# An attention and two-FFN kernel: gate and value of batch 1 from seven products a block instead of eight, and the sums of weights that they need made from the output product of batch 0 on

## The chip, the cores and the metric

The kernel runs on one core of a Trainium2 chip. Its time is the device time of one launch in microseconds (us). Five engines work beside each other, each on its own queue of instructions in a fixed order: TensorE (PE in the profile, its weight loads PEld), VectorE (DVE), ScalarE (ACT), GpSimd (POOL) and SyncE (SP), which here issues the transfers. They wait for each other by semaphores.

## The reference

The reference is an attention with a memory, followed by two feed-forward stages on 4 batches of 576 tokens with 512 channels:

```python
local = softmax(causal(q @ k.T / 8)) @ v                 # 8 heads of 64
mem   = (phi(q) @ M_prev) / (phi(q) @ z_prev + 1e-6)
x     = g * mem + (1 - g) * local                        # 2304 x 512
h     = ((x @ w1) * (x @ w2)) @ w3 @ w_out               # 512 -> 1024 -> 1024 -> 512
out   = (sigmoid(h @ w_gate) * (h @ w_val)) @ w_out2     # 512 -> 1536 -> 512
```

All is float32. Each large product is made of three half- or rounded-precision ones: the operands are split in a high and a low part, and high x high, low x high and high x low are summed.

## The kernel before

**Stages.** Tokens are worked batch by batch, `ffn(b)` for b = 0 to 3, while the attention of batch b + 1 is made in between. w3 and the first w_out are multiplied once into one matrix (prep). A batch then has four stages, which this text calls by product and batch. ab1 is (x w1) * (x w2) of batch 1, 8 blocks of 128 columns. xw1 is the product with w3 w_out, 4 blocks. gv1 is sigmoid(gate) * val, 12 blocks. ot1 is the last product, 4 blocks. The two halves of a batch are 288 tokens each.

**Eight products and seven.** For one block, gate and val (or a and b) are two rows of weights, and the two halves of the tokens are two columns, with two halves of the 512 channels between: a product of 2 x 2 by 2 x 2 blocks, eight products of six matmuls each (2 x 128 channels, 3 parts). `prod` does them plainly. `two_rows` does the same with seven products (Winograd's form): it takes sums of the blocks of the weights ("S") beside the plain blocks ("P"), seven combinations of the blocks of x that `token_steps` makes (named p0 to p6, after the subtractions t1 to t4), and combines the results: two copies on ACT, four additions or subtractions on DVE (L603, L620, L624, L631), one on POOL (L625), sigmoids on ACT and two multiplications on DVE (L594). Before, gv1 is plain, ab and gv of batches 2 and 3 are done by `two_rows`.

**Weights.** In batch 0 the weights are converted, written back in float32 (`kept`) and used at once. Later they are read again, scaled and split to float16: the *late work*, a list of tasks. A task loads a unit of eight 128 x 128 blocks (`late_load`, L298), and `late_split` (L321) does one of its parts at each call: P (ACT makes the high half, DVE the low one, L180 and L181, and it is stored), the sums in place (four DVE instructions, L433 to L436), S (split and stored like P). Before, the list is gate and val P for 12 units, o2 P for 6, a and b P and S for 8 units, gate and val S for 12, o2 S for 6. `pump()` follows the products, and every `pace`-th pump does one part, up to task `limit`. `PACE` has a value for each stage (0: ot0; 5: ab1 and xw1; 1: gv1; 2: ot1; 3: ab2; 4: xw2 and gv2; 6: ot2). `load_step` (L438) brings finished weights from DRAM into a ring of five slots in the order of `again`.

**Order.** The order on TensorE is that of the program's text. On the other engines a scheduler orders the instructions at build time, so a late part stands on DVE's queue where it was expected to fit, and all behind it wait for it. Three PSUM banks (`ps_f`) rotate among the products: the fourth product of a chain waits until the first one's bank has been read.

Of the kernel before, what the change touches and what calls it, by code (L numbers as in the profile page):

```python
# [57 lines left out]
PACE = (4, 4, 4, 14, 4, 8, 4)  # L58
# [5 lines left out]
def tile_attention_memory_ffn(  # L64
# [126 lines left out]
    def unit(src, stage=None, ring=True):  # L191
        u = len(units)
        if stage in plain:
            for hf in range(2):
                n = 2 * u + hf
                stored[n] = dr.tile([128, 2, 4, 128], F32, tag=f"k{n}", name=f"k{n}")
                plain[stage].append((stored[n], [], 4))
        if stage in ("ab", "gv"):
            kept[u] = dr.tile([128, 8, 128], F32, tag=f"kf{u}", name=f"kf{u}")
            nb = 8 if stage == "gv" else 6  # L200
            whole16[u] = {
                "S": dr.tile([128, 2, 8, 128], F16, tag=f"ka{u}", name=f"ka{u}"),
                "P": dr.tile([128, 2, nb, 128], F16, tag=f"kb{u}", name=f"kb{u}"),
            }
# [38 lines left out]
    tasks = [(u, "P") for u in jobs[:F2]] + [(("o", *x), "P") for x in pairs_of]  # L243
# [513 lines left out]
    def ffn(b):  # L757
# [112 lines left out]
        def measure(f):  # L870
            if f == 0 and b == 1:
                for d in range(2):
                    largest(x2top[:, d : d + 1], x2[d][:, 0], AX.X)
            elif f == 1 and b == 1:
                for d in range(2, KC):
                    largest(x2top[:, d : d + 1], x2[d][:, 0], AX.X)
            elif f == 0:
# [11 lines left out]
        def finish_hg(f, ht, hraw):  # L889
# [10 lines left out]

        for f in range(F2):
# [41 lines left out]
            s = take(1 if b else 2)  # L943
            for hf in range(2):
                c0 = hf * HS
                pss = []
                for w in range(2):
                    ps = ps_f.tile([128, 512], F32, tag="f", name=f"gv{b}_{f}_{hf}_{w}")
                    pss.append(ps)
                    for k in range(KC):  # L950
                        prod(ps[:, :HS], *gvw(b, s, w, k), x2[k], c0, k == 0, k == KC - 1)
                        if k % 2 == 1:
                            pump()
                    if w == 0:
# [1 line left out]
                        act_fn(out=asb, in_=ps[:, :HS], func=AF.Sigmoid, scale=x2back[:, f : f + 1] if b else 1.0)
                    if hf == 1 and (b == 0 or w == 1):
                        release(s + (w if b == 0 else 0))
                if b:
                    nc.vector.scalar_tensor_tensor(  # L960
                        hraw[:, c0 : c0 + HS], pss[1][:, :HS], x2back[:, f : f + 1], asb, ALU.mult, ALU.mult
                    )
                else:
                    nc.vector.tensor_mul(hraw[:, c0 : c0 + HS], pss[1][:, :HS], asb)
            if b:
                finish_hg(f, ht, hraw)
            else:
                split_rows(ht, hraw, SHARE_H)
# [79 lines left out]
    def tails(b):  # L1048
# [472 lines left out]
```

## Time and profile before

| what | us |
|---|---|
| median of 3 runs (1017.33 to 1019.17) | 1017.5 |
| the profiled execution | 1020.4 |
| its span, first to last instruction | 1018.6 |
| TensorE busy | 990.1 |
| VectorE busy | 731.5 |
| ScalarE busy | 596.7 |
| GpSimd busy | 194.5 |

The profile is of one execution. Busy time is the union of an engine's instructions; a matmul's end is modelled, so a busy TensorE is not TensorE at its peak, and its progress is better read from when stages start. The mean time of an instruction that the profile gives can overlap the next one's: what a row of ready instructions takes is read from their starts. Idle time of an engine that is waited for by nobody costs nothing.

### The profile page before, as it was taken

The numbers are of one execution on the slowest core, as the hardware profiler recorded it, in microseconds if no ns is written. First come the engines' busy times: TensorE is split into PE (matmuls) and PEld (weight loads), VectorE is DVE, ScalarE is ACT, GpSimd is POOL, SyncE is SP. The second block draws the span as 40 slices with busy tenths as digits, with TensorE's granted clock in tenths as the row PEclk, the third lists the DMA queues.
The fourth block names the chain that finished last, engine by engine and source line by source line (L and its number), as shares of the span: only waits on it lengthen the run. The fifth ranks groups of instructions, "written<-read, shape, count | busy, mean of one in ns | idle before, by whom it ended". The sixth has DMA issues, their size and how long they took to land. (4 is left out here: it accounts for less than half of the span.)

```text
span 1018.6 us, 19895 instructions
## 1 busy us (share of the span) xinstructions
PE 990.1 (97%) x7351; PEld 800.3 (79%) x7351; DVE 731.5 (72%) x1702; ACT 596.7 (59%) x1213; POOL 194.5 (19%) x196
## 2 busy tenths in 40 slices
PE   7999999999999999999999999999999999999998
PEld 3556687888999899898977777778877677797776
DVE  6766788776778826777777668988876757737783
ACT  7987786556777744665655545655645545324451
POOL 3454112203000101312200011343111311201110
PEclk9989999999999999999999999999999999999999
DMA  8775799867677339876988576654655556556532
GB/s 295 229 228 193 248 348 321 316 205 248 215 247 251 122 120 386 270 241 225 294 315 263 184 237 232 227 187 158 213 179 182 190 158 201 182 172 249 182 130 79
DMA packets 95642, 227.21 MB, mean 223 GB/s; under 512 B 11192, under 2 KB 39992, under 8 KB 95288
## 3 DMA queue, kind: packets, MB, share of 16 engines
q1 hardware_dynamic: 95544, 225.93, 66.0%
q8 instruction: 58, 0.95, 0.4%
q14 instruction: 40, 0.33, 0.1%
HBM read 164.55 MB, written 61.34 MB: 222 GB/s over the span
## 5 line engine op out<-in xcount | busy, mean ns | idle before, releaser
L532 PEld LDWEIGHTS <-wslot 128*128 128x128 f16 x1680 | 162.8, 98 | 51.0 <-issue 8.7
L1200 POOL TENSOR_SCALAR p<-p,sm,omg 116x116 f32<-116x116 f32 (+4 forms) x100 | 87.6, 880 | 409.5 <-DVE sm L1198 240.0
L521 PE MATMUL gv<-x,wslot 128*128 128x288 f32 (+1 forms) x1152 | 147.5, 290 | 0.2 <-ACT gsb L137 0.2
L521 PEld LDWEIGHTS <-wslot 128*128 128x128 f16 x1152 | 110.8, 98 | 34.0 <-issue 6.6
L532 PE MATMUL gvp<-x,wslot 128*128 128x288 f16 x1008 | 125.2, 286 | 4.1 <-ACT x L180 1.6
L137 ACT ACTIVATE p<-p,sm 116x116 f32<-116x116 f32 (+4 forms) x160 | 93.0, 584 | 46.6 <-DVE sm L1174 46.5
L521 PE MATMUL ot<-hg,wslot 128*128 128x288 f16 (+1 forms) x864 | 119.3, 291 | 0.0
L521 PE MATMUL ab<-x,wslot 128*128 128x288 f32 x768 | 118.3, 302 | 0.5 <-ACT asb L800 0.4
L521 PE MATMUL xw<-h,wslot 128*128 128x288 f32 x768 | 115.3, 303 | 1.8 <-ACT h L721 1.0
L521 PEld LDWEIGHTS ab<-x,wslot 128*128 128x128 f32 x768 | 104.2, 188 | 8.4 <-issue 4.9
L521 PEld LDWEIGHTS xw<-h,wslot 128*128 128x128 f32 x768 | 105.1, 191 | 6.8 <-issue 3.2
L1174 DVE CUSTOM_DVE_ANT_0 p<-s,msk 116x116 f32<-116x116 f32 (+4 forms) x160 | 68.1, 453 | 31.7 <-PE s L1169 31.0
L532 PE MATMUL abp<-x,wslot 128*128 128x288 f16 x672 | 87.4, 286 | 1.4 <-DVE u2ab L603 1.1
L723 DVE TENSOR_TENSOR wslot<-wraw,wslot 128x512 fp32r<-128x512 f32 x76 | 54.7, 721 | 38.9 <-ACT wslot L721 37.3
L521 PEld LDWEIGHTS gv<-x,wslot 128*128 128x128 f32 x576 | 76.4, 188 | 0.5 <-ACT gsb L137 0.5
L1230 PE MATMUL t<-idf,p 116*116 116x116 f32 x480 | 69.7, 274 | 2.8 <-DVE p L1200 2.2
L1230 PEld LDWEIGHTS t<-idf,p 116*116 116x116 f32 x480 | 55.0, 140 | 17.5 <-issue 4.8
L721 ACT CAST wslot<-wraw 128x512 fp32r<-128x512 f32 x76 | 47.1, 621 | 19.6 <-PE gv L521 7.4
L402 ACT ACTIVATE cy<-r 128x512 f32<-128x512 f32 x76 | 51.4, 676 | 10.8 <-issue 2.2
L411 DVE SCALAR_TENSOR_TENSOR wraw<-cy,cr 128x512 int32<-128x512 int32 x76 | 54.2, 740 | 2.8 <-ACT cr L403 2.4
L1298 PE MATMUL o<-pt,vs 116*64 116x344 f32 (+2 forms) x320 | 51.7, 417 | 0.5 <-ACT pt L1248 0.5
L521 PE MATMUL wps<-wo,wslot 128*128 128x512 f32 x192 | 52.2, 407 | 0.0
(210 smaller groups left out, 1632.6 us busy)
## 6 DMA issues: line engine op xcount, KB each, us to landing
wslot<-k SPq DMA_DIRECT2D x40, 512.0 KB, 4.5
wslot<-ka SPq DMA_DIRECT2D x40, 512.0 KB, 4.6
wrawl<-kf SPq DMA_DIRECT2D x32, 512.0 KB, 6.3
wslot<-kb SPq DMA_DIRECT2D x40, 384.0 KB, 3.6
k<-wslot SPq DMA_DIRECT2D x24, 512.0 KB, 4.7
r<-in_gv_dram SPq DMA_DIRECT2D x24, 512.0 KB, 4.8
kf<-wraw SPq DMA_DIRECT2D x20, 512.0 KB, 3.5
ka<-wS SPq DMA_DIRECT2D x20, 512.0 KB, 4.8
```

The source lines that it names most:

```text
L137: ins = nc.scalar.activation(**kw)
L402: nc.scalar.activation(out=y, in_=hi, func=AF.Prelu, scale=2.0**-112, alpha=2.0**32)
L411: nc.vector.scalar_tensor_tensor(z, y, 3, tmp["r"], ALU.logical_shift_left, ALU.bitwise_or)
L521: paced["pe"] = nc.tensor.matmul(ps, w[:, wi, blk, :], x[:, xi, cols : cols + n], start=first and part == 0, stop=last and part == 2,)
L532: paced["pe"] = nc.tensor.matmul(ps, w[:, wi, blk + k, :], x[:, xi, k, :], start=not more and k == 0 and part == 0, stop=k == 1 and part == 2,
L721: nc.scalar.copy(dst[:, 0], src)
L723: eng.tensor_sub(dst[:, 1], src, dst[:, 0].bitcast(F32))
L1174: nc.vector.tensor_tensor_reduce(out=ps_[hh][:, c0:c1], in0=os_[hh], in1=msk[:, SP - w + c0 : SP - w + c1], scale=-0.125, scalar=3.0e38 if ...
L1200: lower(SHARE_N).tensor_scalar(ps_[hh][:, :w], ps_[hh][:, :w], sm[:, 6 + hh : 7 + hh], omg[:T, 2 * p + hh : 2 * p + hh + 1], ALU.mult, ALU ...
L1230: nc.tensor.transpose(tp[:T, c : c + T], src[hh][:, j * T : (j + 1) * T], idf[:T, :T])
L1298: nc.tensor.matmul(ot[r, XO + q0 : XO + S], v_[:, j, hh], pt[:, hh, j].rearrange("p a c -> p (a c)")[:, q0 - X : S - X] if j < 4 else pt[: ...
```

## The change

gv1 now goes through `two_rows` like gv2 and gv3. So its x2 is no longer split block by block during xw1: xw1's results are kept in float32 (`x2f`) and `token_steps` makes the seven operands at the end of xw1. gv1 loads S (512 KB) and P (now six blocks, 384 KB) for each of 12 units, where it loaded P alone (eight blocks, 512 KB). The list of tasks is now gate and val P and S for 12 units, o2 P for 6, a and b P and S for 8, o2 S for 6; the second pass over gate and val is gone. The paces change, `limit` after gv1 stays at the end of the a and b tasks until batch 2 begins, and `tails` no longer forces the tasks up to there. The lines of the diff that matter:

```diff
-PACE = (4, 4, 4, 14, 4, 8, 4)
+PACE = (2, 5, 3, 14, 8, 3, 8)
...
-            nb = 8 if stage == "gv" else 6
...
-                "P": dr.tile([128, 2, nb, 128], F16, tag=f"kb{u}", name=f"kb{u}"),
+                "P": dr.tile([128, 2, 6, 128], F16, tag=f"kb{u}", name=f"kb{u}"),
...
-    tasks = [(u, "P") for u in jobs[:F2]] + [(("o", *x), "P") for x in pairs_of]
+    tasks = [(u, "PS") for u in jobs[:F2]] + [(("o", *x), "P") for x in pairs_of]
     NFIRST = len(tasks)
     tasks += [(u, "PS") for u in jobs[F2:]]
     NPARTS = len(tasks)
-    tasks += [(u, "S") for u in jobs[:F2]]
-    NSUMS = len(tasks)
     tasks += [(("o", *x), "S") for x in pairs_of]
...
-    again = plain["ab"] + plain["xw"] + gv8 + ot8
+    again = plain["ab"] + plain["xw"] + gv16 + ot8
...
         if b == 2:
-            ws["pace"] = PACE[3]
+            ws["limit"], ws["pace"] = len(tasks), PACE[3]
...
-        if b == 1:
-            x2s = bound_x2(b, htop)
-        if b > 1:
+        if b > 0:
             xf = [fp.tile([128, 2, S], F32, tag=f"h{10 + n}", name=f"x2f{b}_{n}", bufs=1) for n in range(2)]
...
-                elif b == 1 and d == 0:
-                    nc.scalar.copy(x20[:, c0 : c0 + HS], ps[:, :HS])
-                elif b == 1:
-                    split_scaled(xt[:, 0, c0 : c0 + HS], xt[:, 1, c0 : c0 + HS], ps[:, :HS], x2s[:, 0:1])
...
-            if b == 2:
+            if b:
                 for _ in two_rows(
                     take(2), x2, f"gv{b}_{f}", hraw[:, :HS], hraw[:, HS:], x2back[:, f : f + 1], True
                 ):
                     pass
...
         if b == 1:
-            ws["limit"], ws["pace"] = NSUMS, PACE[2]
+            ws["pace"] = PACE[2]
         if b == 2:
-            ws["limit"], ws["pace"] = len(tasks), PACE[6]
+            ws["pace"] = PACE[6]
...
         def first():
-            late_until(NPARTS)
             nc.vector.tensor_reduce(mx, xmax[b], AX.X, ALU.max)
```

The order on TensorE is the same outside gv1 and the last block of xw1 (whose two halves change places). On VectorE it shifts in all stages from ot0 to ot2. In ab1, at the end of block 2, it had this before (wP is the low half of a P split, hraw the product of a and b, htop its largest value; sm, p and qkl belong to the attention of batch 2):

```order
L1087 TENSOR_TENSOR qkl2_1_5195<-qk2_1_4872,qkh2_1_5194 128x580
L1197 TENSOR_SCALAR sm2_0_4_5123<-sm2_0_4_5123 116x2
L1198 RECIPROCAL sm2_0_4_5123<-sm2_0_4_5123 116x2
L1200 TENSOR_SCALAR p2_0_4_0_5121<-p2_0_4_0_5121,sm2_0_4_5123,omg_91 116x580
L181 SCALAR_TENSOR_TENSOR wP6_5211<-wrawl_6_4854,wsc_83,wP6_5211 128x1024
L803 TENSOR_TENSOR hraw1_2_5094<-ab1_2_1_1_5177,asb1_2_1_5175 128x288
L176 TENSOR_REDUCE htop1_4827<-hraw1_2_5094 128x1
```

and it has this now, in the same place (wS is the low half of an S split, wrawl the sums, h the split of hraw; lines of the changed file are lower by 4 to 38):

```order
L1049 TENSOR_TENSOR qkl2_1_5233<-qk2_1_4888,qkh2_1_5232 128x580
L432 TENSOR_TENSOR wrawl_4_4799<-wrawl_4_4799 128x256
L1159 TENSOR_SCALAR sm2_0_4_5151<-sm2_0_4_5151 116x2
L1160 RECIPROCAL sm2_0_4_5151<-sm2_0_4_5151 116x2
L794 TENSOR_TENSOR hraw1_2_5120<-ab1_2_1_1_5211,asb1_2_1_5209 128x288
L1162 TENSOR_SCALAR p2_0_4_0_5149<-p2_0_4_0_5149,sm2_0_4_5151,omg_91 116x580
L176 TENSOR_REDUCE htop1_4841<-hraw1_2_5120 128x1
L181 SCALAR_TENSOR_TENSOR wS4_5168<-wrawl_4_4799,wsc_83,wS4_5168 128x1024
L181 SCALAR_TENSOR_TENSOR wP5_5219<-wrawl_5_4900,wsc_83,wP5_5219 128x768
L714 TENSOR_TENSOR h1_2_5119<-hraw1_2_5120,h1_2_5119 128x576
```

Where one whole P split (wP6) stood, there are now a sum, an S split and a P split: about one task of P, sums and S goes to a block. In gv1, blocks 5 and 6, VectorE had before (hgraw is sigmoid(gate) * val of one half, hg its split):

```order
L960 SCALAR_TENSOR_TENSOR hgraw1_5_6722<-gv1_5_0_1_6740,x2back1_6022,gsb1_5_0_6738 128x288
L181 SCALAR_TENSOR_TENSOR wP21_6788<-wrawl_21_6529,wsc_83,wP21_6788 128x768
L960 SCALAR_TENSOR_TENSOR hgraw1_5_6722<-gv1_5_1_1_6775,x2back1_6022,gsb1_5_1_6773 128x288
L433 TENSOR_TENSOR wrawl_21_6529<-wrawl_21_6529 128x256
L434 TENSOR_TENSOR wrawl_21_6529<-wrawl_21_6529 128x256
L181 SCALAR_TENSOR_TENSOR hg1_5_6721<-hgraw1_5_6722,hgs1_6557,hg1_5_6721 128x576
L435 TENSOR_TENSOR wrawl_21_6529<-wrawl_21_6529 128x256
L436 TENSOR_TENSOR wrawl_21_6529<-wrawl_21_6529 128x256
L960 SCALAR_TENSOR_TENSOR hgraw1_6_6796<-gv1_6_0_1_6814,x2back1_6022,gsb1_6_0_6812 128x288
L181 SCALAR_TENSOR_TENSOR wS21_6860<-wrawl_21_6529,wsc_83,wS21_6860 128x1024
L960 SCALAR_TENSOR_TENSOR hgraw1_6_6796<-gv1_6_1_1_6847,x2back1_6022,gsb1_6_1_6845 128x288
```

and now, blocks 4 and 5 (u2gv and u3gv are the additions and subtractions of `two_rows`, L590 its multiplications, L594 before):

```order
L599 TENSOR_TENSOR u2gv1_4_6790<-gvp1_4_6_6779,s1gv1_4_6777 128x288
L181 SCALAR_TENSOR_TENSOR hg1_3_6686<-hgraw1_3_6687,hgs1_6672,hg1_3_6686 128x576
L429 TENSOR_TENSOR wrawl_19_6500<-wrawl_19_6500 128x256
L616 TENSOR_TENSOR u3gv1_4_6815<-gvp1_4_6_6779,s1gv1_4_6777 128x288
L430 TENSOR_TENSOR wrawl_19_6500<-wrawl_19_6500 128x256
L620 TENSOR_TENSOR u2gv1_4_6790<-gvp1_4_5_6792,u2gv1_4_6790 128x288
L431 TENSOR_TENSOR wrawl_19_6500<-wrawl_19_6500 128x256
L627 TENSOR_TENSOR u3gv1_4_6815<-u3gv1_4_6815,gvp1_4_4_6826 128x288
L432 TENSOR_TENSOR wrawl_19_6500<-wrawl_19_6500 128x256
L590 SCALAR_TENSOR_TENSOR hgraw1_4_6767<-s5gv1_4_6799,x2back1_6094,u2gv1_4_6790 128x288
L590 SCALAR_TENSOR_TENSOR hgraw1_4_6767<-u3gv1_4_6815,x2back1_6094,c11gv1_4_6807 128x288
L599 TENSOR_TENSOR u2gv1_5_6864<-gvp1_5_6_6857,s1gv1_5_6855 128x288
```

A block has six instructions of its own ahead of its split where it had two, and the late parts stand between them.

## Rows read from the trace of the kernel before

**Rows 1.** The page's part 1: busy us, share of the span, instructions.
```profile
PE 990.1 (97%) x7351; PEld 800.3 (79%) x7351; DVE 731.5 (72%) x1702; ACT 596.7 (59%) x1213; POOL 194.5 (19%) x196
```

**Rows 2.** Timeline of TensorE, gv1: start us, us, engine, line, what, count.
```profile
504.79 17.81 PE L521 MATMUL gv<-x,wslot 128*128 128x288 f16 x144
...
522.46 53.08 PE L521 MATMUL gv<-x,wslot 128*128 128x288 f16 x432
575.38 0.53 PE L521 MATMUL ot<-hg,wslot 128*128 128x288 f16 x3
```

**Rows 3.** Timeline of TensorE, gv2; in brackets idle before, and what ended it.
```profile
727.72 1.15 PE L532 MATMUL gvp<-x,wslot 128*128 128x288 f16 x8
...
733.67 0.41 PE L532 MATMUL gvp<-x,wslot 128*128 128x288 f16 x2 [0.76 <-ACT x L180]
...
749.80 42.79 PE L532 MATMUL gvp<-x,wslot 128*128 128x288 f16 x348 [0.31 <-ACT s5gv L608]
792.42 0.53 PE L521 MATMUL ot<-hg,wslot 128*128 128x288 f16 x3
```

**Rows 4.** Windows: stretch, us, busy PE, PEld, DVE, ACT, POOL, clock, DMA share, GB/s.
```profile
339.00:391.00 52.00, 50.84 (x374) 46.50 (x374) 24.19 (x51) 25.37 (x44) 6.00 (x4) 0.97 0.42 143
391.00:472.00 81.00, 80.67 (x624) 69.99 (x624) 60.16 (x160) 48.47 (x109) 22.07 (x20) 1.00 0.80 278
472.00:505.00 33.00, 33.00 (x257) 30.96 (x256) 24.12 (x64) 18.88 (x40) 8.78 (x7) 1.00 0.84 266
505.00:575.50 70.50, 70.50 (x578) 56.30 (x577) 51.98 (x90) 39.27 (x55) 0.00 (x0) 1.00 0.78 266
575.50:628.00 52.50, 51.18 (x420) 37.27 (x418) 35.97 (x79) 26.73 (x46) 5.00 (x5) 1.00 0.66 217
...
728.00:792.50 64.50, 62.38 (x506) 49.15 (x504) 49.37 (x103) 33.72 (x65) 9.52 (x12) 1.00 0.58 192
```

**Rows 5.** Groups of DVE, whole span: count | busy us, mean ns | idle before.
```profile
L181 DVE SCALAR_TENSOR_TENSOR wS<-wrawl,wsc,wS 128x1024 f16<-128x1024 f32 x20 | 26.0, 1301 | 6.5 <-ACT wS L180 6.4
...
L181 DVE SCALAR_TENSOR_TENSOR hg<-hgraw,hgs,hg 128x576 f16<-128x576 f32 x24 | 19.5, 816 | 2.8 <-ACT hg L180 2.6
...
L960 DVE SCALAR_TENSOR_TENSOR hgraw<-gv,x2back,gsb 128x288 f32<-128x288 f32 x24 | 12.4, 516 | 11.6 <-PE gv L521 9.5 <-PE hgsum L172 1.5 <-ACT gsb L137 0.4
...
L603 DVE TENSOR_TENSOR u2gv<-gvp,s1gv 128x288 f32<-128x288 f32 x24 | 11.0, 456 | 4.0 <-ACT s1gv L599 1.2 <-PE gvp L532 1.0
...
L181 DVE SCALAR_TENSOR_TENSOR wP<-wrawl,wsc,wP 128x768 f16<-128x768 f32 x8 | 8.1, 1010 | 2.5 <-ACT wP L180 2.5
...
L594 DVE SCALAR_TENSOR_TENSOR hgraw<-s5gv,x2back,u2gv 128x288 f32<-128x288 f32 x12 | 6.1, 512 | 0.0
```

**Rows 6.** Timeline of DVE in gv2.
```profile
748.99 1.54 DVE L181 SCALAR_TENSOR_TENSOR hg<-hgraw,hgs,hg 128x576 f16<-128x576 f32 x2
750.45 0.45 DVE L620 TENSOR_TENSOR u3gv<-gvp,s1gv 128x288 f32<-128x288 f32 x1
750.81 0.45 DVE L624 TENSOR_TENSOR u2gv<-gvp,u2gv 128x288 f32<-128x288 f32 x1
...
762.20 0.51 DVE L594 SCALAR_TENSOR_TENSOR hgraw<-s5gv,x2back,u2gv 128x288 f32<-128x288 f32 x1
762.62 0.51 DVE L594 SCALAR_TENSOR_TENSOR hgraw<-u3gv,x2back,c11gv 128x288 f32<-128x288 f32 x1
```

**Rows 7.** One line's sums: min/median/max ns, first in gv1, then in ot1.
```profile
L433 DVE TENSOR_TENSOR wrawl<-wrawl x7: 414/415/417, 515.3 to 567.3; 128x256 f32<-128x256 f32 x7
...
L433 DVE TENSOR_TENSOR wrawl<-wrawl x6: 414/419/1645, 582.1 to 622.9; 128x256 f32<-128x256 f32 x6
```

**Rows 8.** What TensorE waited for: us in total, times, longest us.
```profile
PE xsum L172 <- DVE bcol L1056: 1.9, 2, 1.3
...
PE gvp L532 <- DMA wslot<-kb: 0.7, 1, 0.7
```

**Rows 9.** Groups of DVE in ab1, 391 to 472 us.
```profile
L181 DVE SCALAR_TENSOR_TENSOR wP<-wrawl,wsc,wP 128x1024 f16<-128x1024 f32 x9 | 11.8, 1314 | 8.8 <-ACT wP L180 8.7
```

More of the change, by code (lines that the diff above doesn't have):

```diff
@@ L253, in tile_attention_memory_ffn @@
     )
-    gv8 = [(whole16[u]["P"], [(u, "P")], 8) for u in jobs[:F2]]
     ot8, ot16 = (
@@ L713, in out_rows @@
                 store(1, 0, u3)
-    def gvw(b, s, w, k):
-        m = (k + 2 * w) % 4
-        return (slot(s), 4 * w + m) if b else (slot(s + w), m)
     def split_rows(dst, src, share=None):
@@ L821, in ffn @@
                 x2back = finish_x2(b, x2s)
-                if b == 1:
-                    split_scaled(x2[0][:, 0], x2[0][:, 1], x20, x2s[:, 0:1])
             s = take(2)
-            if b < 2:
-                xt = fp.tile([128, 2, S], F16 if b else F32R, tag=f"x{d}", name=f"x2_{b}_{d}", bufs=1)
+            if b == 0:
+                xt = fp.tile([128, 2, S], F32R, tag=f"x{d}", name=f"x2_{b}_{d}", bufs=1)
                 x2.append(xt)
-            if b == 1 and d == 0:
-                x20 = fp.tile([128, S], F32, tag="hraw", name="x20")
-            for n, hf in enumerate((1, 0) if b > 1 and d == KC - 1 else (0, 1)):
+            for n, hf in enumerate((1, 0) if b > 0 and d == KC - 1 else (0, 1)):
                 c0 = hf * HS
@@ L859, in ffn @@
         hs = []
-        if b == 1:
-            x2top = fp.tile([128, 8], F32, tag="x2top", name=f"x2top{b}", bufs=1)
         if b == 3:
@@ L870, in measure @@
         def measure(f):
[L871 to L877, printed above, removed]
+            if f == 0:
                 for n, m in enumerate((0, 1, 5, 4)):
@@ L882, in measure @@
             elif f == 2:
-                return hg_scale(b, x2top[:, : 4 if b == 1 else 8], x2s)
+                return hg_scale(b, x2top, x2s)
         if b == 1:
@@ L897, in finish_hg @@
                 split_scaled(ht[:, 0], ht[:, 1], hraw, hgs[:, 0:1])
-                if b == 1:
-                    flush(1)
         for f in range(F2):
@@ L942, in ffn @@
                 continue
-            s = take(1 if b else 2)
+            s = take(2)
             for hf in range(2):
@@ L950, in ffn @@
                     for k in range(KC):
-                        prod(ps[:, :HS], *gvw(b, s, w, k), x2[k], c0, k == 0, k == KC - 1)
+                        prod(ps[:, :HS], slot(s + w), (k + 2 * w) % 4, x2[k], c0, k == 0, k == KC - 1)
                         if k % 2 == 1:
@@ L955, in ffn @@
                         asb = fp.tile([128, HS], F32, tag="asb", name=f"gsb{b}_{f}_{hf}")
[L956 to L968, printed above, removed]
+                        act_fn(out=asb, in_=ps[:, :HS], func=AF.Sigmoid, )
+                    if hf == 1:
+                        release(s + w)
+                nc.vector.tensor_mul(hraw[:, c0 : c0 + HS], pss[1][:, :HS], asb)
+            split_rows(ht, hraw, SHARE_H)
         yield 0.0
```

## The prediction

> **What bounds the kernel now.** I read the page's busy times first, then what TensorE waited for, its timeline, and the engines' work stage by stage. TensorE works 990.1 of 1018.6 us and VectorE (DVE) 731.5 [rows 1], so the kernel is a chain of TensorE stages, and time is won where a stage has fewer matmuls. I call the stages by product and batch: ab1, xw1, gv1 and ot1 are batch 1's four, gv2 the third of batch 2. The change makes gv1 what gv2 is already, so the trace holds its model. gv1 runs from 504.79 us until ot1 begins at 575.38: 70.59 us for 144 + 432 matmuls, 122.6 ns each, no wait before any [rows 2]. gv2 runs from 727.72 to 792.42: 64.70 us for 504, with four waits, the longest of 0.76 us; its steady part does 348 matmuls in 42.79 us, so a block of 42 takes 5.16 us [rows 3]. Next to TensorE stands DVE: busy 60.16 of 81 us in ab1, 24.12 of 33 in xw1, 51.98 of 70.5 in gv1, 35.97 of 52.5 in ot1 and 49.37 of 64.5 in gv2, and just 24.19 of 52 in ot0 [rows 4]. The change loads just this engine in ab1, xw1 and gv1, so its room there decides.
>
> **gv1, the matmuls.** 12 blocks x 48 matmuls become 12 x 42. The 72 that go are worth 72 x 122.6 ns = 8.8 us. The start of seven products costs some of it back, since the operands of products 6, 2, 5, 7, 3 and 4 are sums over all of xw1; gv2 shows that price in its waits. Stage against stage the change is 64.70 - 70.59 = -5.9 us, if DVE keeps up as in gv2.
>
> **gv1, DVE in a steady block.** Before, a block has two multiplications of 516 ns (hgraw from gv) and one split of 816. After, it has four additions or subtractions of about 456, two multiplications of about 512 and the same split: 4 x 0.456 + 2 x 0.512 + 0.816 = 3.66 us at full durations [rows 5]. Instructions that stand ready start before the last one ends: two splits take 750.45 - 748.99 = 1.46 us, an addition 750.81 - 750.45 = 0.36, a multiplication 762.62 - 762.20 = 0.42 [rows 6]. Packed, the block is 4 x 0.36 + 2 x 0.42 + 0.73 = 3.0 us. Beside it, one part of the late work of ab2's weights comes every fifth of the 84 products (PACE[1] 4 to 5): a P split (1.010 us for six blocks), four sums of about 0.42 and an S split (1.30) make a task of 15 products, 2.14 blocks [rows 5, 7]. That is 3.99 us a task, 1.86 a block. DVE has then 4.9 us (packed) to 5.5 us (full) to do in a block in which TensorE works 5.16. At the packed end it is free, at the full end it costs 0.36 x 8 = 2.9 us over the eight steady blocks. I take 1.2, nearer the packed end, because DVE works through the dense stretch around 750 us almost packed.
>
> **gv1, blocks 2 and 3.** There stand, by the order, the last two of the four largest-value reductions, the chain for hgs, three splits of hg, a whole late task and both blocks' own work: 31 rows, about 15.0 us at full durations and 12.5 packed, against 10.3 us of TensorE. The excess is 2.2 to 4.7 us. TensorE may run ahead of DVE by two products (three banks rotate, and u3's addition frees the one that the next block begins with): 12 x 122.6 ns = 1.5 us. That leaves 0.7 to 3.2; I take 1.7. So gv1 gives -5.9 + 1.2 + 1.7 = -3.0 us. The six blocks of S and P that are loaded per block where four were taken (896 KB for 512) run behind a ring of five slots; I cost them at nothing, and where that cover is gone the wait is of the size of the one that the trace has, 0.7 us [rows 8].
>
> **ab1 and xw1.** By the order, ab1 has 8 whole P splits before, and after 7 shorter ones, 8 S splits and 28 sums. With 1.314 for the whole P split [rows 9] and the prices above, DVE loses 8 x 1.314 = 10.5 us and gains 7 x 1.01 + 8 x 1.30 + 28 x 0.42 = 29.2: 60.2 + 18.7 = 78.9 of 81 us at full durations, or 76.1 when each of the 35 more starts 0.08 us before the last one ends, as the packed prices have it. Sums can also be held by GpSimd (POOL): in ot1, where POOL is busy 5.00 of 52.5 us, one of 24 sums took 1645 ns where its line's median is 419; in gv1, with POOL idle, the same line's stay at 417 or under [rows 4, 7]. In ab1 POOL is busy 22.07 of 81 us [rows 4], 2.9 times that share, so 28 sums meet it 28/24 x 2.9 = 3.4 times, 4.1 us. That makes 80.2 of 81. The bounds are 0, if packing covers it, and 8.2, if DVE waits for ScalarE as it does now (the rival below). I take +1.0, by the row near which the sum ends: full, but not over. In xw1 DVE gains 7 to 9 us (two tasks with sums and S splits, and part of x2's four sums and three more splits) on 24.12 of 33: it just fits, at nothing; if not, the excess goes into gv1's start.
>
> The Trainium skill, page "SBUF — State Buffer", section "Who interferes with whom", says that a VectorE instruction with both inputs in SBUF and a GpSimd instruction that reads SBUF lock each other out for a whole instruction. The 1645 ns sum of ot1 agrees. By that rule the 15 splits count beside the 28 sums, 43/24 x 2.9 x 1.23 = 6.4 us for 4.1, and ab1 stands at 82.5 of 81; the slack of 1.5 us would still hold it. Without the rule ab1 would cost nothing and the sum below would be one microsecond better.
>
> **ot0, gv2 and the rest.** In ot0, three P splits, twelve sums and two S splits stand where four P splits stood, 10.7 us for 5.3, on an engine that is over half idle there: nothing. In gv2, tasks of w_out's sums now come every eighth product; blocks 2 and 3 hold about 12.8 us (mean of packed and full) for 10.3, less the 1.5 of slack, 1.0, against the wait of 0.31 for s5 that stands there now [rows 3]: +0.7 (0 to 1.9, if DVE holds them for all of their work). ot1, xw2 and ot2 lose late work (about 6, 5 and 17 us of DVE). Little of it was in TensorE's way: of the 1.9 us that it waits for the scale of the next batch [rows 8], one sum of about 0.4 us goes in ot1; -0.5 (0 to -1.9).
>
> The sum: -3.0 + 1.0 + 0.7 - 0.5 = -1.8 us. Against the profiled execution (1020.4 us, span 1018.6) that is 1018.6; that execution lay 2.9 us over the median of 1017.5, so against the median 1015.7.
>
> **The rivals.** (B) DVE keeps up everywhere: -5.9 us, 1011.6. For it speaks how densely DVE can run, and that ab1's and gv1's work is known well ahead of its need; against it, blocks 2 and 3 of gv1 that exceed TensorE even packed. (C) Slower: in ab1 each split's second half goes on waiting for its first half from ScalarE. Now DVE idles 8.7 us before 9 of them, 0.97 each [rows 9]. Fifteen at that price are 14.6; 76.1 + 14.6 = 90.7 is 9.7 over 81, 8.2 after the slack, and the sum -3.0 + 8.2 + 0.7 - 0.5 = +5.4: 1022.9. It costs from 81 + 1.5 - 76.1 = 6.4 us of such waiting on, and makes the kernel slower than before from 2.8 more, 9.2 us or 0.61 a split. Against it: DVE idled there because it had nothing else, and a later DVE finds the half made. (D) The gain is eaten inside gv1: full durations, 2.9 + 3.2 in place of 1.2 + 1.7, gives +0.2 there and with the other terms +1.4: 1018.9. For it speaks that the reductions and the splits of hg stand in the way whatever else moves; against it the dense stretch of gv2, which runs packed. That the change does not do what it says, the sums being late for gv1, the order speaks against: all twelve tasks of gv's weights stand on DVE ahead of gv1's first block.
>
> **How the numbers follow.** My forecast (A, between -4 and 0) gets 0.42, B 0.25, C 0.18, D 0.15. A measurement of this kernel tells no change from one beyond about 0.2%, 2.0 us. Of A 0.20 falls under faster, 0.20 under the same, 0.02 under slower; B is faster; D is the same with 0.11 and slower with 0.04; C is slower: 0.45, 0.31, 0.24. The range goes from B's time, a little under, 1011.3, up to 1021.5, which leaves out most of C. A's own range is 1013.5 to 1017.5.
>
> **What would show it.** Right: gv1 of about 67.5 us with 504 products and blocks 2 and 3 over 5.16 us long; DVE over 75 of 81 us busy in ab1 and over 60 in gv1; TensorE's new waits there ended by DVE (u2gv, u3gv). B is shown by a gv1 under 65.5 us. C by ab1 over 84 us with DVE idle before the splits, ended by ScalarE. D by gv1 at 70 us. Wrong would be a wait for the new slots' transfers of several us, or a gain in a stage whose work did not change.

## The result, and the profile after

The changed kernel takes 1027.99 us (median of 4 runs, 1027.29 to 1029.65), the kernel before 1018.05 beside it: a ratio of 1.0100, 95% interval 1.0075 to 1.0125. It is slower by about ten microseconds; the forecast was 1015.7, and its range ended at 1021.5. The spans of the two profiled executions are 1025.8 and 1018.6 us.

The page after, part 1, answers to [rows 1]: TensorE has 5 us less to do, VectorE (DVE) 26.5 us more.

```profile
PE 985.1 (96%) x7279; PEld 792.5 (77%) x7279; DVE 758.0 (74%) x1754; ACT 605.9 (59%) x1243; POOL 210.3 (21%) x208
```

The windows of the stages answer to [rows 4], with the same columns; the stretches are ot0, ab1, xw1, gv1, ot1 and ab2.

```profile
338.00:387.90 49.90, 48.74 (x371) 44.56 (x370) 27.88 (x59) 26.08 (x45) 6.04 (x4) 1.00 0.43 148
387.90:476.70 88.80, 83.48 (x625) 70.99 (x625) 80.38 (x199) 53.41 (x115) 23.33 (x20) 0.98 0.80 275
476.70:510.20 33.50, 33.13 (x256) 30.98 (x255) 30.71 (x71) 23.59 (x45) 7.81 (x6) 1.00 0.87 291
510.20:583.70 73.50, 65.77 (x507) 49.80 (x505) 67.01 (x131) 42.40 (x77) 12.86 (x13) 0.98 0.86 301
583.70:635.90 52.20, 51.22 (x421) 37.29 (x419) 33.70 (x71) 28.43 (x48) 5.93 (x6) 1.00 0.61 196
635.90:697.50 61.60, 58.83 (x481) 43.12 (x480) 54.78 (x145) 34.45 (x85) 25.89 (x23) 1.00 0.60 190
```

From the first matmul of a stage to the first of the next, ab1 goes from 81.1 to 88.7 us, gv1 from 70.6 to 73.6 with 72 matmuls fewer, and ab2 from 59.7 to 61.5; xw1 is 0.5 longer. Back come 0.3 in ot1, 0.9 each in ot2, ab3 and gv3. That is +10.1; the rest of the difference of the spans, -2.9, lies ahead of ab1, where stretches at the lower clock fall elsewhere from one execution to the next.

What TensorE waited for, from 380 to 700 us (us in total, times, longest us), answers to [rows 8]. Before, the same stretch had four waits with 2.6 us in all, of which 0.2 were for t. A wait for a slot's transfer, which the prediction priced at up to 0.7, is there once, with 0.4. All else that is new ends with DVE or with ScalarE, but for 0.4 us of GpSimd's part of p.

```profile
PE t L1192 <- DVE p L1162: 5.0, 5, 1.8
PE gvp L528 <- DVE x L181: 2.9, 3, 1.1
PE gvp L528 <- ACT s5gv L604: 1.5, 2, 1.1
PE abp L528 <- DVE u3ab L627: 1.4, 1, 1.4
PE hgsum L172 <- DVE bcol L990: 1.1, 1, 1.1
...
PE gvp L528 <- DMA wslot<-kb: 0.4, 1, 0.4
```

The first line is ab1, all but 0.3 us of it. There TensorE computes, beside the feed-forward layer of batch 1, the attention of a later batch: scores s go to DVE, to ScalarE's exponential, back to DVE (sum, reciprocal, p), and then TensorE transposes p into t. The timelines of TensorE and then of DVE show the longest of these waits.

```profile
462.26 0.36 PE L1131 MATMUL s<-qkh 64*116 64x232 f32 x2
...
462.76 0.67 PE L517 MATMUL ab<-x,wslot 128*128 128x288 f32 x3
465.22 0.38 PE L1192 MATMUL t<-idf,p 116*116 116x116 f32 x2 [1.80 <-DVE p L1162]
```

```profile
461.42 0.16 DVE L1160 RECIPROCAL sm<-sm 116x2 f32<-116x2 f32 x1
461.49 1.83 DVE L181 SCALAR_TENSOR_TENSOR wP<-wrawl,wsc,wP 128x768 f16<-128x768 f32 x1
463.25 0.39 DVE L1136 CUSTOM_DVE_ANT_0 p<-s,msk 116x232 f32<-116x232 f32 x1
...
463.88 1.19 DVE L1162 TENSOR_SCALAR p<-p,sm,omg 116x116 f32<-116x116 f32 x1
```

The reciprocal that the last p needs is there at 461.58, but the split wP, a late part, stands ahead and lasts 1.83 us beside GpSimd, and the step of the next scores comes ahead too: p starts at 463.88, 2.3 us late, and t gets it at 465.07. TensorE has three matmuls of its own to do in that time. Not all of it is order: the same split takes 1.01 us elsewhere in ab1, and p itself 0.34 where GpSimd is idle, so 1.7 us of the 3.5 from the reciprocal to the end of p are instructions that last longer beside GpSimd's:

```profile
393.18 0.34 DVE L1162 TENSOR_SCALAR p<-p,sm,omg 116x116 f32<-116x116 f32 x1
```

```profile
463.60 1.40 POOL L714 TENSOR_TENSOR h<-hraw,h 128x576 fp32r<-128x576 f32 x1
```

The next longest wait, 1.49 us at 405.25, is almost all order. Between its reciprocal and its p stand three instructions of the kernel's own and one late sum (0.50 us): here DVE is behind with its own work too.

```profile
402.48 0.16 DVE L1160 RECIPROCAL sm<-sm 116x2 f32<-116x2 f32 x1
...
404.74 0.45 DVE L1162 TENSOR_SCALAR p<-p,sm,omg 116x348 f32<-116x348 f32 x1
```

Behind the longest wait comes a second price. Two windows around it:

```profile
461.50:465.50 4.00, 2.20 (x19) 1.72 (x18) 4.00 (x9) 1.90 (x6) 3.50 (x3) 1.00 1.02 351
465.50:468.90 3.40, 3.40 (x16) 1.96 (x14) 3.02 (x11) 0.35 (x1) 0.59 (x1) 0.50 0.66 245
```

TensorE was busy for 2.20 of 4.00 us, and then for 3.4 us its granted clock is 0.50, that is 1.2 GHz for 2.4: 1.7 us more are lost, though nothing waits. The same happens in gv1 at 520.1 us. For ab1 the account is 81.0 us of work, 5.3 of waits and 1.7 of clock, 88.0 of the 88.7.

gv1 starts like this, to be compared with gv2's [rows 3], where the longest wait is 0.76:

```profile
512.57 1.63 PE L528 MATMUL gvp<-x,wslot 128*128 128x288 f16 x12 [1.06 <-DVE x L181]
515.03 2.12 PE L528 MATMUL gvp<-x,wslot 128*128 128x288 f16 x16 [0.83 <-DVE x L181]
517.97 0.41 PE L528 MATMUL gvp<-x,wslot 128*128 128x288 f16 x2 [0.81 <-ACT x L180]
519.42 12.82 PE L528 MATMUL gvp<-x,wslot 128*128 128x288 f16 x88 [1.05 <-DVE x L181]
533.30 0.16 PE L172 MATMUL hgsum<-bcol,ones 128*128 128x1 bf16 x1 [1.06 <-DVE bcol L990]
...
538.29 2.37 PE L528 MATMUL gvp<-x,wslot 128*128 128x288 f16 x18 [1.12 <-ACT s5gv L604]
```

Against gv2's 64.7 us, 8.9 too many: waits are 7.7 for 2.1 (+5.6), the clock 1.7, and 1.6 remain that no record names.

### The profile page after: what moved, and what is told of

It is laid out like the page before. It is cut to its first block, busy times and chain, and to the rows that moved or that the text cites. A ratio compares the mean times of both kernels' runs of the same rounds, so it can differ in the third digit from the quotient of the medians.

```text
span 1025.8 us, 19867 instructions
## 1 busy us (share of the span) xinstructions
PE 985.1 (96%) x7279; PEld 792.5 (77%) x7279; DVE 758.0 (74%) x1754; ACT 605.9 (59%) x1243; POOL 210.3 (21%) x208
## 4 chain that ended last, share of the span: by engine, by line
PE 68%; DVE 17%; ACT 5%; DMA 5%; issue 3%; POOL 1%; SPq 0%; DVEq 0%; POOLq 0%; ACTq 0%
PE gvp L528 12%; PE ot L517 9%; PE xw L517 8%; PE gv L517 7%; PE ab L517 6%; PE abp L528 6%; PE s L1131 5%; PE o L1260 4%; PE t L1192 3%; PE wps L517 3%; PE o L1245 2%; DVE p L1136 2%; PE otp L650 2%; DVE hg L181 1%; DMA wpart<-wp 1%
## 5 line engine op out<-in xcount | busy, mean ns | idle before, releaser
L528 PEld LDWEIGHTS <-wslot 128*128 128x128 f16 x2184 | 212.6, 98 | 74.5 <-issue 19.7
L528 PE MATMUL gvp<-x,wslot 128*128 128x288 f16 x1512 | 191.0, 287 | 9.9 <-DVE x L181 3.8
L1162 POOL TENSOR_SCALAR p<-p,sm,omg 116x116 f32<-116x116 f32 (+4 forms) x100 | 88.9, 894 | 349.7 <-DVE sm L1160 223.0
L517 PE MATMUL gv<-x,wslot 128*128 128x288 f32 x576 | 76.7, 295 | 0.2 <-ACT gsb L137 0.2
L621 POOL TENSOR_TENSOR s5gv<-u3gv,s5gv 128x288 f32<-128x288 f32 x36 | 31.7, 880 | 199.6 <-DVE u3gv L616 183.3
L517 PEld LDWEIGHTS <-wslot 128*128 128x128 f16 x576 | 54.5, 98 | 19.5 <-issue 6.3
```

What stands on the lines that cost most here:

```text
L517: paced["pe"] = nc.tensor.matmul(ps, w[:, wi, blk, :], x[:, xi, cols : cols + n], start=first and part == 0, stop=last and part == 2,)
L528: paced["pe"] = nc.tensor.matmul(ps, w[:, wi, blk + k, :], x[:, xi, k, :], start=not more and k == 0 and part == 0, stop=k == 1 and part == 2,
L1162: lower(SHARE_N).tensor_scalar(ps_[hh][:, :w], ps_[hh][:, :w], sm[:, 6 + hh : 7 + hh], omg[:T, 2 * p + hh : 2 * p + hh + 1], ALU.mult, ALU ...
```

## The experiments

The theories are three: **V**, DVE is too full or works in a bad order, and TensorE waits behind it; **T**, the transfers of the late work (loads of raw tiles, stores of splits, slots) hold the stages; **S**, gv1's loss is its start alone. Ratios are against the kernel before on the same chip; a stage's length is that of the one profiled execution of each kernel.

**Without the sums.** The four DVE sums of each late task of gate, val, a and b are left out, so the S operands are not what the kernel needs.

```
-            sums(raw, nc.vector, nc.vector)
+            if late_o2:
+                sums(raw, nc.vector, nc.vector)
```

> The changed kernel without the four sums (VectorE) in the late tasks of gate, val, a and b; the S splits are then made of plain blocks, so the results of gv1 to gv3 and ab2, ab3 are not the reference's. All transfers stay. Theory V (VectorE is full in ab1 and gv1, so its work sets their length): VectorE has some 12 us less in ab1 and 8 less in gv1; ab1 goes from 88.9 us to 81 to 83, gv1 from 73.8 to 66 to 68, the time from 1028 to 1013 to 1017. Theory T (transfers: the late work's stores and the larger slots hold the stages): ab1 and gv1 stay within 1 us, the time within 2 us of 1028.

1022.34 us, ratio 1.0023 (1.0004 to 1.0043): of the ten microseconds 6 by the medians and 8 by the ratios go with the sums, so V has a share, but the expected 1013 to 1017 is missed. gv1 is 69.4 us. ab1 is 86.6 us with DVE busy 66.6, because of one wait, and 6.8 us at the lower clock around its end. ScalarE's record ahead of that wait and TensorE's:

```profile
394.28 1.15 ACT L180 ACTIVATE wS<-wrawl,wsc 128x1024 f16<-128x1024 f32 x1 [0.95 <-DMA kb<-wP]
```

```profile
399.51 0.70 PE L1193 MATMUL t<-idf,p 116*116 116x116 f32 x2 [2.72 <-DVE sm L1160]
```

ScalarE works in order too: a split that waits for its tile (an earlier split's store must leave it) holds the exponentials behind it. Its 0.95 us are a part of the 2.72: DVE, too, has other instructions between the reciprocal (397.58) and p (398.65).

**More transfers.** One more copy of 512 KB in memory for each late load.

```
+            behind(nc.sync.dma_start(out=again_dr[n % 4], in_=kept[u]))
```

> The changed kernel with one more transfer for each late load: the same 512 KB once more, from DRAM to a scratch tile in DRAM that nothing reads (32 of them, about 1 MB of traffic each). Theory V: ab1 and gv1 keep their length within 1 us and the time stays within 3 us of 1028. Theory T: the transfer engines' share is 0.8 to 1.1 in these stages already, so they grow by 5 us or more together and the time passes 1033.

1036.73 us, 1.0181 (1.0159 to 1.0202); ab1 91.8, gv1 79.3. V expected next to nothing here and is wrong on it; the sizes are those of T. What is new in gv1 is named by its waits:

```profile
PE gvp L530 <- DMA wslot<-kb: 6.4, 2, 3.6
```

In the changed kernel that line has 0.4. So transfers are not what it waits for, but their cover is thin: the DMA share in gv1 is 0.86, and at 0.94 it is gone. In ab1 no wait ends with a transfer; why those for t grow there (6.8 us of idle TensorE for 5.3, 6.8 us at the lower clock for 3.4) is open.

**Spread otherwise.** `PACE` from (2, 5, 3, 14, 8, 3, 8) to (2, 8, 2, 14, 8, 4, 8).

> The changed kernel with the paces (2, 8, 2, 14, 8, 4, 8): fewer late parts in ab1 (by the order 20.5 us of VectorE work for 28.2), xw1 and gv1 (13.2 for 20.6), more in ot1 (25.7 for 12.8), where VectorE is a third idle, and in ab2 (10.8 for 5.7). Theory V: ab1 82 to 84 us, gv1 67 to 70, ot1 52 to 54, ab2 62 to 64, the time 1015 to 1020. Theory T: the same bytes move, only later; 1025 or more. Theory S (the start of seven products in batch 1 and its waits are the loss, not VectorE's load): gv1 stays above 72 us, ab1 above 87, 1026.

1027.55 us, 1.0081 (1.006 to 1.0103); the total that V expected is missed, and lies where T and S had it. ab1 84.2 and gv1 67.9 are as V said; but the work that left them came due in ab2, which goes to 68.6 us with DVE 63.8 busy. In these three stages the length followed the load, and moving it only helps where there is room.

**The moved work alone.** gv1 in eight products as before, with the changed list of late tasks and its paces.

> Half of the change: the kernel before, with gv1 in eight products, but with the changed list of tasks (P and S of gate and val together, P still of eight blocks) and the changed paces. Theory V: ab1 as long as in the changed kernel or longer, 88 to 92 us, since VectorE has by the order 76 us of work there for 73; gv1 as before, 70 to 71; the time 1026 to 1030, so the whole loss comes from the moved work, and seven products in gv1 bring nothing beside it. Theory S: 1016 to 1020, and the seven products lose 8 us or more.

1035.78 us, 1.0171 (1.015 to 1.0192). ab1 takes 96.0 us (10.0 of waits, all but 0.4 for t, and 10.2 us at the lower clock), gv1 71.3. The loss is larger than expected, and it stands in ab1 without any seven products in gv1. The change is some 7 us faster than this kernel, but not by its seven products: its gv1 is 2.3 us longer (73.6), and its ab1 is 7.3 shorter, where its P splits are of six blocks and not of eight.

**DVE alone.** The kernel before, with idle additions on DVE: no transfer, no ScalarE work, no data waited for.

```
+        if more["pace"] and more["pumps"] % more["pace"] == 0:
+            for _ in range(5):
+                behind(nc.vector.tensor_add(idle, idle, idle))
```

> The kernel before, with idle additions put on VectorE and nothing else: in ab1 12 groups of five (128 x 192, some 0.34 us each, about 20 us), in gv2 10 such groups (17 us). No transfer, no ScalarE work and no wait for data is added, so it tells VectorE's load from the transfers. Theory V (VectorE works in order, and what TensorE waits for stands behind the late work): ab1 goes from 81.1 to 85 to 88 us, with new waits of TensorE ended by VectorE's p and sm; gv2 from 64.7 to 67 to 71; the kernel 1024 to 1031. Theory T (the late work's loads, stores and ScalarE halves hold the stages): ab1 stays at 81 to 82, gv2 at 65 to 66, the kernel at 1018 to 1021.

1026.07 us, 1.0078 (1.0048 to 1.0109). Windows of ab1 and gv2:

```profile
387.40:476.30 88.90, 83.06 (x626) 70.80 (x625) 80.36 (x223) 48.67 (x108) 22.34 (x20) 0.98 0.74 257
732.20:798.40 66.20, 62.99 (x507) 49.28 (x506) 62.06 (x153) 33.08 (x64) 9.48 (x12) 1.00 0.55 187
```

ab1's whole loss is back, to 0.2 us, with the very same DVE time (80.36 for the change's 80.38). So T is not needed for ab1: more work on DVE alone is enough to lose as much. That the sizes agree so closely is in part luck, because the waits are not the same ones. In the change they end with DVE's part of p; here most end with the part that GpSimd makes from DVE's reciprocal:

```profile
PE t L1242 <- POOL p L1212: 3.9, 3, 1.8
```

For the longest of them the reciprocal is there at 424.50. GpSimd then makes another operand (me) first, and its part of p behind it:

```profile
424.86 1.82 POOL L1124 TENSOR_TENSOR me<-mphi,z 116x640 f32<-116x640 f32 x1 [5.63 <-DVE idle L369]
426.66 0.54 POOL L1212 TENSOR_SCALAR p<-p,sm,omg 116x116 f32<-116x116 f32 x1
```

In the kernel before, p stands first:

```profile
424.23 1.14 POOL L1200 TENSOR_SCALAR p<-p,sm,omg 116x116 f32<-116x116 f32 x1 [5.41 <-DVE sm L1198]
425.34 1.56 POOL L1112 TENSOR_TENSOR me<-mphi,z 116x640 f32<-116x640 f32 x1
```

The additions have shifted the order on GpSimd too. No run here adds load and keeps all orders, or takes GpSimd's hold on DVE away, so the shares of load, order and that hold in the 7.8 us are not shown. gv2 is another matter: 12.4 us more of DVE cost it 1.5 us, less than expected.

**The sums on GpSimd.**

```
-            sums(raw, nc.vector, nc.vector)
+            sums(raw, nc.gpsimd, nc.gpsimd)
```

> The changed kernel with the four sums of each late task on GpSimd instead of VectorE: same transfers, same splits, same order. Theory V: VectorE's busy time falls by about 11 us in ab1 and 8 in gv1, ab1 comes to 82 to 84.5 us, gv1 to 67 to 69, the kernel to 1013 to 1018. Theory L (GpSimd's work on the same memory holds VectorE, or delays GpSimd's own share of p behind the sums): VectorE's instructions get longer by what was taken off, or TensorE waits for POOL's p; ab1 87 us or more, the kernel 1025 to 1035. Theory T: as the changed kernel, 1026 to 1029.

1035.63 us, 1.0157 (1.0121 to 1.0194): worse than the change, and at the end of L's range (1035). ab1 is 88.4 us and xw1 39.4. DVE's time in ab1 falls by 6.8 us to 73.5; without any sums (above) the same 167 instructions took 66.6, so 6.9 come back as longer instructions. The Trainium skill, page "SBUF — State Buffer", section "Who interferes with whom", says that a VectorE instruction with two inputs in SBUF and a GpSimd one that reads SBUF exclude each other. The trace agrees: one split of 1.30 us took 1.61 beside a sum on GpSimd of 1.59 (c2 below, at 395 us). But the largest part is the twelve small steps sm of the softmax (116 x 2, one tile read), 5.5 us for 2.0. TensorE's longest waits end with DVE's sm (3.5 us, in ab1) and with ScalarE (3.6 us, in xw1); the next kernel shows how ScalarE comes to be late.

**GpSimd and fewer turns.** Sums right behind the first split of their task, `PACE` (2, 10, 3, 14, 8, 5, 8).

> A candidate: the changed kernel with the sums on GpSimd, issued right behind the first split of their task, and fewer turns of late work (every fifth pump in ab1 and xw1, every tenth in gv1, every third in ot1), so that by the order VectorE holds some 63 us of work in ab1 and 54 in gv1 where the changed kernel holds 73 and 66. Theory V: ab1 81 to 83 us, gv1 66 to 67.5, no loss in ot1 and ab2, the kernel 1009 to 1014, faster than both. Theory L: little better than the changed kernel, 1020 to 1028. Theory T: 1024 to 1028, since all transfers stay.

1031.04 us, 1.0114 (1.0076 to 1.0152), outside all three expectations; ab1 92.6 us. ScalarE, GpSimd and TensorE around one of its waits:

```profile
425.69 1.15 ACT L180 ACTIVATE wS<-wrawl,wsc 128x1024 f16<-128x1024 f32 x1 [2.29 <-POOL wrawl L435]
426.74 0.92 ACT L180 ACTIVATE wP<-wrawl,wsc 128x768 f16<-128x768 f32 x1
427.57 0.38 ACT L137 ACTIVATE p<-p,sm 116x116 f32<-116x116 f32 x1
```

```profile
431.86 0.42 PE L1195 MATMUL t<-idf,p 116*116 116x116 f32 x1 [3.36 <-ACT p L137]
433.60 0.45 PE L1195 MATMUL t<-idf,p 116*116 116x116 f32 x1 [1.33 <-POOL p L1165]
```

ScalarE stands for 2.29 us at a split whose sums GpSimd has not finished, and the exponential comes behind two splits; DVE's half of the first is late with it. GpSimd's own share of p comes behind its sums and its me as well (the second wait). Taking load off DVE gave the wait to two other engines that work in order.

**Late work held off at gv1's start.**

```
+            if b == 1 and d == KC - 1:
+                ws["pace"] = 0
```

(and the pace of gv1 set at its third block)

> The changed kernel without late work from the last row of xw1 to the second block of gv1: by the order, five splits (P of tasks 13 to 17) that stand among and behind the splits of x2 on VectorE move some ten blocks later; in all 2.7 us of VectorE's work leave gv1 and 6.6 go to ot1. Theory S (gv1's loss is a matter of place: the seven operands of x2 are late because splits of weights stand between them): the waits ended by x (3.7 us in the changed kernel) and the stretch at the lower clock go, gv1 from 73.6 to 68.5 to 71 us, the kernel 1023 to 1026. Theory V (a matter of mean load): gv1 72 to 73, the kernel 1026 to 1028.

1026.94 us, 1.0065 (1.0042 to 1.0088); gv1 70.7 us, as S said, its lines of waits now these:

```profile
PE gvp L528 <- DVE u2gv L599: 2.7, 6, 0.5
PE hgsum L172 <- DVE bcol L992: 1.1, 1, 1.1
...
PE gvp L528 <- DVE x L181: 0.4, 1, 0.4
```

The 3.7 us of waits for x become 1.2, and the stretch at the lower clock is gone. That is 2.9 of gv1's 8.9; the other 6 are not at its start. The whole gains less (1 us by the medians, 3.5 by the ratios) and lies in V's range, not in S's: ab2 gives back 0.7.

**Three candidates.** c2: sums on GpSimd, S splits one task later. c3: sums on GpSimd from gv1 on only. c4: the change with turns by load, `PACE` (2, 6, 2, 100, 8, 5, 8) and 2 in xw1. All hold late work off at gv1's start and keep o2's S tasks out of ab2.

> The sums on GpSimd again, but the S split of a task comes behind the P split of the next one, so that the sums have a whole turn more before ScalarE comes to them; the late work held off at gv1's start as in e8; o2's S tasks kept out of ab2 and made with sums on VectorE. If the loss with GpSimd came from ScalarE standing at a split for its sums (2.3 us, with the softmax's exponentials behind it): ab1 82 to 84.5 us, gv1 66 to 68, the kernel 1008 to 1014. If it came from the two engines' hold on each other or from GpSimd's own late p: ab1 86 or more, the kernel 1018 to 1026.

> A candidate: late sums on VectorE in ot0, ab1 and xw1, on GpSimd from gv1 on (no softmax there); S splits one task behind their sums; the late work held off at gv1's start; every seventh pump in ab1 (by the order 66 us of VectorE's work there, 53.5 in gv1, 39 in ot1, 50 in ab2). By place and load together: ab1 83 to 85, gv1 66 to 67.5, ot1 52.5 to 53.5, ab2 59.5 to 60.5: 18 to 14 us under the changed kernel, 1010 to 1015. If every change of placement only moves the waits elsewhere: 1022 to 1028.

> A candidate with the sums on VectorE as in the change, spread by load alone: turns every fifth pump in ab1, every second in xw1, held off at gv1's start, then every sixth, every second in ot1, none of o2's tasks in ab2. By the order 62.6 us of VectorE's work in ab1 (the changed kernel 73.3), 34.0 in xw1 (32.2), 59.0 in gv1 (65.6), 45.4 in ot1 (31.5), 52.0 in ab2 (55.6). By load: ab1 82 to 84, xw1 33.5 to 35, gv1 67 to 68.5, ot1 53.5 to 55, ab2 59.5 to 61: the kernel 1012 to 1019. If every change of placement only moves the waits elsewhere: 1022 to 1028.

c2: 1027.57 us, 1.0094 (1.0059 to 1.0129). gv1 is 66.2, as expected, but ab1 89.9 with DVE only 69.3 busy. ScalarE's waits for the sums, 8.0 us in c1's ab1, are gone, and one wait of 3.5 us for DVE's sm is left: the lag did not free the chain, and ScalarE's standing was not the whole cause. That is the second expectation (ab1 86 or more), with a time over its 1026. c3: 1036.90, 1.0159 (1.0126 to 1.0192); gv1 67.1, but ot1 64.6 (12 us lost, with a wait of 3.8 us in the attention and one of 4.0 for the scale of the next batch), past both expectations. c4: 1022.22, 1.0029 (1.0002 to 1.0055), 6 to 7 us better than the change: ab1 83.6, gv1 67.6, ab2 61.1, as expected by load, and xw1 37.5, which is not. The time is where the waits were only to move, 1022 to 1028. xw1 has one wait and the clock behind it:

```profile
PE t L1196 <- DVE p L1166: 2.5, 1, 2.5
```

```profile
501.50:504.90 3.40, 0.92 (x9) 0.56 (x7) 3.40 (x13) 2.22 (x7) 1.27 (x2) 1.00 1.02 364
504.90:508.30 3.40, 3.36 (x15) 3.39 (x16) 2.86 (x3) 1.69 (x3) 1.33 (x1) 0.50 1.00 366
```

**The same work in shorter instructions.** Each late split in two halves; e9 is the change so cut, c5 is c4, and c7 is c5 with turns every third pump in xw1.

```
-            for ins in split_scaled(t[:, 0], t[:, 1], raw[:, :nb], by):
-                behind(ins)
+            for c in (slice(0, nb // 2), slice(nb // 2, nb)):
+                for ins in split_scaled(t[:, 0, c], t[:, 1, c], raw[:, c], by):
+                    behind(ins)
```

> The changed kernel with each late split in two halves, on ScalarE and VectorE alike: the same elements, transfers and turns, 40 more instructions on VectorE in all (about 3 us from ot0 to ab2), but the longest one that can stand ahead of a softmax step there is 0.7 us instead of 1.3, and 0.6 on ScalarE instead of 1.15. If the length of the single instruction sets the waits: TensorE's waits in ab1 fall from 5.3 to 2 or 3 us and the stretch at the lower clock goes, ab1 84 to 86.5 us, gv1 71 to 73, the kernel 1020 to 1024. If the load sets them: ab1 88 to 90, gv1 73 to 75, the kernel 1028 to 1031.

> The even spread (c4) with the splits in halves. If the length of the single instruction sets the waits: ab1 82 to 83, xw1 33 to 34.5 (37.5 in c4, with a wait of 2.5 us and a stretch at the lower clock behind it), the kernel 1014 to 1019. By load: 1022 to 1026.

> As c5, with turns every third pump in xw1 instead of every second: some 5 us less of late work there, on gv1, ot1 and ab2 instead. If xw1's wait in c4 came of the late work's density there: xw1 33 to 33.5, gv1 67.5 to 69, the kernel 1013 to 1018. If the waits move with every placement, whatever its load: one of 2 to 4 us somewhere else from ab1 to ab2, the kernel 1020 to 1026.

e9: 1027.86 us, 1.0089 (1.0055 to 1.0124), the change's time. At 79.9 us of DVE, ab1's waits go from 5.3 to 4.4 us, not to 2 or 3; ab1 is 85.5 because this execution has no stretch at the lower clock there. So the load sets most of the waits, the length of the single instruction little. c5: 1021.20, 1.0017 (0.9998 to 1.0036), the best version with seven products, not told apart from the kernel before; ab1 84.2 and xw1 35.6 miss the 82 to 83 and 33 to 34.5 of shorter instructions, and the time lies between the two ranges. c7: 1027.71, 1.0078 (1.0053 to 1.0103): xw1 still has a wait of 1.6 us with 3.4 us at the lower clock, and gv1 (70.5) and ab2 (64.4) have new ones, the longest of 3.3 us. So waits came elsewhere with the placement, as its second expectation said, if not in place of the old one; the time is over its 1026.

## Why the prediction was wrong

**The step that failed** is the term of ab1: "I take +1.0, by the row near which the sum ends: full, but not over." What the load does was wrong: +7.6. The step treats a stage as free until its second engine is full, and no row gives the +1.0. In its place TensorE waited for 5.3 us, nearly all of it for p, which came late from DVE, and lost 1.7 us at the lower clock. The upper bound of 8.2 covers the loss, but it was made for DVE's waiting, not for TensorE's.

The load itself came out, 80.2 us of DVE forecast and 80.4 measured, but partly by luck. 32 sums and 8 P splits run there, not 28 and 7. GpSimd held one of the sums, for 0.4 us, where 3.4 holds of 4.1 us were taken; it held splits and the softmax's own steps instead. In all, 11 of DVE's instructions in ab1 last over 0.25 us longer than others of their form, 7.9 us together, where before it was 5 and 3.4 us.

Side by side, ab1 in all kernels whose late sums there are on DVE or that have none:

| kernel | DVE busy, us | TensorE's waits | at the lower clock | ab1 |
|---|---|---|---|---|
| before | 60.0 | 0.3 | 0 | 81.1 |
| without the sums | 66.6 | 3.0 | 6.8 | 86.6 |
| c5, even, halves | 69.3 | 2.0 | 3.4 | 84.2 |
| c4, even | 70.4 | 2.6 | 0 | 83.6 |
| c7, halves | 70.5 | 2.5 | 3.4 | 84.8 |
| c3 | 72.3 | 5.8 | 6.8 | 89.2 |
| spread otherwise | 74.7 | 2.9 | 0 | 84.2 |
| halves | 79.9 | 4.4 | 0 | 85.5 |
| more transfers | 79.9 | 6.8 | 6.8 | 91.8 |
| held off at gv1 | 80.2 | 5.4 | 3.4 | 88.8 |
| changed | 80.4 | 5.3 | 3.4 | 88.7 |
| before, idle additions | 80.4 | 5.8 | 3.4 | 88.9 |
| moved work alone | 82.5 | 10.0 | 10.2 | 96.0 |

The length is 81 plus the waits plus half the time at the lower clock, to within 1 us. The waits grow from far below a full engine. The row to read was in [rows 4]: DVE was a quarter idle in ab1, and that let a softmax step start soon after its input came. Late work takes the idle time, and each of two visits to DVE in the chain can then find it busy. The table doesn't tell load from place entirely: c3 waits 5.8 us at 72.3, and the kernel without sums 3.0 at 66.6. Nor does it tell either from GpSimd's hold, which made up about half of the time that p was late at the longest wait.

**gv1, -3.0 forecast, +3.0 measured.** The matmuls went as counted. Against the model of gv2 the prediction added 2.9 us for DVE; the stage came to 8.9 over it. The start was taken from gv2 unchanged, but in gv1 five P splits of tasks 13 to 17 stand among and behind x2's: 2.9 us, clock included, as holding them off showed. Blocks 2 and 3 cost 2.4 us of waits where 1.7 was taken for them. DVE's load explains part of the rest: gv1 takes 66.2 us at 53.5 us of DVE (c2), 67.6 at 58.6 (c4), 70.7 at 62.1 (held off), 73.0 at 69.8 (halves). But gv2 with idle additions took 66.2 at 62.1, so load alone isn't it: late splits also load ScalarE and the transfers. What share each has is open.

**Smaller terms.** xw1 at nothing: +0.5. gv2 +0.7: +0.1. ot1 and ot2, -0.5: -1.2, and ab3 and gv3 gave 1.7 that the sum did not have. ab2, which it did not have either, lost 1.8. Transfers at nothing: right, 0.4 us.

**The rivals.** C had the sign and came nearest in time (1022.9), but not by its mechanism: in ab1 DVE stood 0.4 us before splits for ScalarE, where C wanted 0.97 each. Its price was put on DVE's waiting; it was TensorE that waited, behind a DVE that did not. D, the gain eaten inside gv1, came too and went further, +3.0 where it had +0.2, but it was the smaller part of the loss. By the rule of the Trainium skill (page "SBUF — State Buffer", section "Who interferes with whom") that the prediction weighed, splits are held like sums, and DVE would have stood at 82.5 us in ab1. It stood at 80.4. Splits were held there indeed, three of 16 by over 0.25 us, 2.0 us together; the size was not, and DVE's time was not what failed.

Against the change, a version with its work spread by load (c5) is 7 to 8 us faster; no version here beat the kernel before.

## What to carry to other kernels

An engine that serves a chain TensorE waits for has no room up to 100%: ask of each late piece which step of the chain it may stand ahead of, and price the waits from the idle share that goes, not from the excess over the stage. Work taken off TensorE must be weighed against what its replacement costs on the engine that does it, in the stages where that work must stand. Before such a change, put idle instructions of the same time there, and read the stage's length and which waits are new. Moving work to a third engine that works in order can move the wait with it.

## What the runs showed of the hardware

A stretch at 1.2 GHz follows waits that a timeline makes look small: in ab1 1.80 us in one piece (2.20 of 4.00 us busy), in gv1 0.83, 0.81 and 1.05 within 5.3 us (1.63 of the last 3.5 us busy). The stretches lasted 3.4, 6.8 and 10.2 us, the last ahead of ab1 alone, and by the sum below the table they cost about half of that. It isn't sure to come: the change's wait of 1.49 us in ab1 had none behind it, and of six waits of 1.77 to 1.86 us in ab1 (changed, held off, idle additions, halves, c5, c7) the one in halves had none. Nor had two as long elsewhere, 1.81 us in gv1 without the sums and 1.86 in c7's ab2.

VectorE's instructions can take longer beside GpSimd's. The same idle addition, min/median/max ns in ab1, with GpSimd busy 22.3 of 88.9 us, and in gv2, with 9.5 of 66.2:

```profile
L369 DVE TENSOR_TENSOR idle<-idle x63: 334/352/1605, 389.8 to 470.5; 128x192 f32<-128x192 f32 x63
```

```profile
L369 DVE TENSOR_TENSOR idle<-idle x50: 338/350/601, 739.6 to 797.5; 128x192 f32<-128x192 f32 x50
```

It isn't the ones that read two tiles alone: in the changed kernel's ab1 a step sm (116 x 2, one tile read) took 1.40 us at 394.54 where 0.17 is its median, until GpSimd's me was done at 395.92. All 11 of the long instructions there run beside one of GpSimd.

One kernel's time varies by 5 us and more from run to run (c4: 1017.4 to 1025.4), and the profiles differ as much ahead of ab1, where TensorE's instructions are the same in all: ab1 starts at 384.7 us in c5, with 6.8 us at the lower clock until then, and at 392.5 in the kernel held off, with 23.9. Stages are to be compared, not spans.
